# Sliding-window attention with a token mixer: two batches of natural q and k, eight sets of exponentials, held stores and a new order of work

## The chip, the core and the metric

The kernel runs on one core of a Trainium2 chip. Five engines work side by side, each through its own list of instructions in order: TensorE (PE; its weight loads are listed apart as PEld), VectorE (DVE), ScalarE (ACT), GpSimd (POOL) and SyncE (SP). They wait for each other through semaphores only. The metric is the time of one execution on the device in microseconds.

## The reference: what is computed

q, k and v are 8 batches x 8 heads x 576 positions x 64, in float32. Each head has a window of 128 positions and a slope; the attention's output, put side by side over the heads, is x (8 x 576 x 512), and x goes through a token mixer:

```python
scores = scale * np.matmul(q, k.transpose(0, 1, 3, 2))
mask = (rel >= 0) & (rel < window)
scores = np.where(mask, scores + bias[None], -1000000000.0)
...
attn = attn / (np.sum(attn, axis=-1, keepdims=True) + 1e-09)
return np.matmul(attn, v).astype(np.float32)
...
wq = x @ w_q
wk = x @ w_k
W_tok = scale * np.einsum('bsd,btd->bst', wq, wk)
mixed = np.einsum('bst,btd->bsd', W_tok, x)
return (np.maximum(mixed, 0.0) @ w_out).astype(np.float32)
```

The mixer needs the whole of a batch's x before its first product is complete.

## The kernel before

The 576 positions of a batch are four blocks of 128 and a tail of 64. The kernel is a list of small operations, each named after its kind, batch and part (QK3.1.0 is batch 3, block 1, half 0 of the heads). `ORDER` is a text written out beforehand: it gives the operations one after the other, each with its engine (P, A, D, G, S for PE, ACT, DVE, POOL, SP) and, for a PE operation, the pair of PSUM banks and the bank that it fills. Every engine gets its operations in the order of that text and runs them in that order; the framework adds the waits that the data need. The durations and start times that the operations carry in the code (`want`, `pe(...)`, `EV(...)`) were used to make the text and have no effect on a run.

The kinds, in the order in which a batch goes through them:

- Lq, Lk, Lv, Lt: loads of a block of q, of k, of v, and of the tails of two batches, with conversion to float16, issued by GpSimd (POOL). LF are the first blocks, issued by SP and ACT in float32.
- TQ (TF, TJ for batch 0; TT for tails): transposes of a block of q and k on PE; ETQ (EF, EJ, ETT) copies the result from PSUM to `qkT`, on ACT or DVE.
- QK: the scores of one block of keys for four heads, into a pair of banks; EXP (ACT) takes the exponential into a tile `pt`; MUL (DVE) multiplies it by the exponential of the bias, which holds the mask too. `NPT` is the number of sets of `pt` that are used in turn: EXP of a set waits for the products (PV) that read it last.
- PV: the product with v, whose tile has a column of ones, so that the sum comes with it; RC takes its reciprocal and X scales it into `x` (both DVE).
- XT, XTT: transposes of x and of its tails; EXT, EXTT copy them.
- For each two batches: WQ, WK, WT are the products with w_q and w_k (EWQ, EWK, EWT their copies), G is wk times x (EG), MX the mixing with RM and RMT the relu behind it, OUT the product with w_out, EO the copy of the result to a tile `osb`, and DO its store, issued by SP. There are `OSB` tiles `osb` in turn.
- wz, Lw, Lwo, CWQ, CW: wz (DVE) writes one column of the `osb` tile that w_q and w_k are then loaded into, so that SP's load Lw comes behind it; SP issues Lw (two DMAs) and Lwo, the four blocks of w_out; CWQ and CW convert them. WK and WQ need CWQ, OUT needs all CW.
- WM: matmuls on a tile of zeros whose result is not used; `WARM` holds how many of them each stands for.

The operations of a stage are mixed with those of others: while two batches go through the mixer, the next ones go through the attention. Natural q and k (`nat`) and v (`vt`) have room for four batches each; a load waits for the operation that last read what it overwrites. A load that GpSimd issues also waits for the eighth load before it.

Of the kernel before, what the change touches and what calls it, by code (L numbers as in the profile page):

```python
# [25 lines left out]
NNAT = 4  # L26
NV = 4
NPT = 5
# [13 lines left out]
EF0.1.0:D zeros:D Lk0.3:G TF0.0.0:P00 WM.2:P10 EF0.0.0:A TF0.0.1:P01 WM.3:P20 Lt0:G EF0.0.1:A  # L42
QK0.0.0:P1 TF0.1.1:P00 EXP0.0.0:A WM.4:P20 EF0.1.1:D TJ0.1.1:P01 QK0.0.1:P2 WM.5:P30 MUL0.0.0:D
# [4 lines left out]
EXP0.3.0:A MUL0.2.0:D Lv0.1:G WM.11:P01 TQ1.1:P00 EXP0.3.1:A Lq1.3:G MUL0.3.0:D WM.12:P20  # L48
ETQ1.1:D EXP0.2.1:A Lk1.3:G TQ1.0:P01 WM.13:P20 Lv0.2:G ETQ1.0:D MUL0.1.0:D QK1.0.0:P0 Lv0.3:G
QK1.0.1:P1 MUL0.2.1:D PV0.0:P2 EXP1.0.1:A WM.14:P31 Lk2.3:G MUL0.3.1:D TQ1.2:P30 EXP1.0.0:A  # L50
WM.15:P31 ETQ1.2:D Lk2.2:G PV0.1:P1 QK1.1.1:P3 RC0.1:D Lq2.2:G QK1.1.0:P0 X0.1:D EXP1.1.0:A
RC0.0:D Lv1.0:G MUL1.0.0:D TQ1.3:P10 WM.16:P11 EXP1.1.1:A ETQ1.3:D Lq2.3:G PV0.2:P0 X0.0:D
QK1.2.0:P1 Lv1.1:G PV0.3:P3 MUL1.1.0:D EXP1.2.0:A QK1.2.1:P2 MUL1.1.1:D Lv1.2:G EXP1.2.1:A
QK1.3.1:P1 RC0.2:D MUL1.0.1:D Lv1.3:G EXP1.3.1:A MUL1.2.0:D QK1.3.0:P2 Lk2.1:G X0.2:D EXP1.3.0:A
XT0.0:P10 RC0.3:D Lq2.1:G PV1.0:P0 X0.3:D EXT0.0:A MUL1.3.0:D TQ2.3:P11 Lq2.0:G TQ2.2:P20
MUL1.2.1:D ETQ2.3:A PV1.1:P3 Lk2.0:G MUL1.3.1:D XT0.1:P21 RC1.0:D PV1.2:P1 RC1.1:D Lv1.4:G
# [6 lines left out]
CW.3:A QK2.3.0:P1 EG0:D EXP2.3.0:A CW.0:D Lv2.3:G MX0.1:P0 MX0.0:P2 RM1.1:D MX0.3:P3 RM0.1:A  # L63
MX0.2:P1 Lv2.0:G RM1.3:A RM0.3:D TQ3.0:P00 RM1.0:A Lk3.3:G QK2.2.1:P3 ETQ3.0:D RM1.2:A TQ3.1:P01
EXP2.2.1:A RM0.2:D Lv2.2:G OUT1.0:P00 ETQ3.1:D RM0.0:A Lv3.0:G QK2.3.1:P1 MUL2.2.0:D QK3.0.0:P3
EXP2.3.1:A QK3.0.1:P2 MUL2.3.0:D Lk4.2:G OUT1.3:P01 MUL2.0.1:D EXP3.0.1:A OUT1.1:P10 Lk4.1:G
MUL2.3.1:D EXP3.0.0:A MUL2.2.1:D OUT0.1:P11 Lt2:G MUL2.0.0:D EO1.3:A TQ3.2:P20 EO1.0:A
MUL3.0.0:D PV2.1:P3 EO0.1:A ETQ3.2:D Lq4.2:G PV2.0:P0 DO1.0:S TQ3.3:P21 EO1.1:A RC2.1:D
OUT0.3:P11 X2.1:D Lv3.1:G ETQ3.3:A RC2.0:D PV2.3:P3 X2.0:D Lq4.1:G EO0.3:A QK3.1.0:P2 RC2.3:D
QK3.2.0:P0 X2.3:D EXP3.1.0:A Lv3.2:G PV2.2:P1 MUL3.0.1:D OUT1.2:P30 EXP3.2.0:A Lv3.3:G  # L70
MUL3.1.0:D XT2.0:P31 RC2.2:D Lv3.4:G EO1.2:A MUL3.2.0:D QK3.1.1:P2 QK3.3.0:P0 EXP3.1.1:A Lk4.3:G
X2.2:D OUT0.0:P30 EXT2.0:D Lq4.3:G EXP3.3.0:A QK3.3.1:P1 QK3.2.1:P2 EO0.0:D TT4:P31 Lq4.0:G
EXP3.2.1:A MUL3.1.1:D MX0.4:P0 OUT0.2:P30 MUL3.3.0:D RMT0:A Lk4.0:G PV3.0:P2 MUL3.2.1:D
EXP3.3.1:A TQ4.2:P00 Lv2.4:G ETT4:D TQ4.1:P01 ETT5:A RC3.0:D MUL3.3.1:D PV3.1:P1 Lq5.0:G EO0.2:A
# [36 lines left out]
EXT7.0:A DO4.0:S X6.4:D XT7.1:P01 OUT5.2:P20 RC7.4:D EXT7.1:A X7.4:D MX4.4:P3 XTT6:P21 RMT4:D
WK6:P00 EXTT6:A WT6:P01 EWK6:A WQ6:P10 EWT6:D G6:P11 EWQ6:A EO5.2:A OUT5.4:P30 EG6:D DO5.2:S
# [46 lines left out]
def kernel(  # L159
# [751 lines left out]
```

## Time and profile before

| | |
|---|---|
| time of 3 runs, median (lowest to highest) | 143.82 us (143.59 to 145.14) |
| the profiled execution's own time | 145.0 us |
| its span, first to last instruction | 143.1 us |
| PE busy; useful matmuls end | 129.3 us; 138.9 us |
| ACT busy; DVE busy; POOL busy | 118.7; 117.5; 95.3 us |
| warm matmuls | 72, 12.0 us |
| first load of GpSimd; end of its last | 2.46; 106.6 us |
| first exponential starts | 6.99 us |
| first store of a result; last one issued | 54.0; 139.6 us |

Of this profile the busy times by stretch say which engine has room in which stage, the waits say who stood for whom, the chain of work that ended last says where the end comes from, and the timeline gives the moment of a single operation. Durations of instructions that follow each other on an engine overlap by some hundredths of a microsecond, so that a sum of durations is larger than the busy time.

### The profile page before, as it was taken

The page shows a single profiled execution, that of the slowest core. Times are in us where ns is not written, and L with a number is a line of the kernel's source. Part 1 is how long each engine was busy: PE and PEld are TensorE (multiplying, and loading weights), DVE is VectorE, ACT ScalarE, POOL GpSimd, SP SyncE. Part 2 cuts the span into 40 slices and gives each one's busy share as a digit, 9 for nine tenths or more (in the row PEclk, how much of TensorE's full clock was granted, in tenths as well). Part 3 has the DMA queues.
Part 4 walks back from the last instruction along what each step waited for, and adds up shares of the span by engine and source line. Part 5 has one row for each costly group of instructions (what it writes and reads, how often), then busy time and mean ns, then how long its engine had stood idle before and what let it go on. Part 6 is the DMA issues. An engine that isn't in the chain of part 4 may idle for free.

```text
span 143.1 us, 4562 instructions
## 1 busy us (share of the span) xinstructions
PE 129.3 (90%) x1888; PEld 86.8 (61%) x1888; DVE 117.5 (82%) x253; ACT 118.7 (83%) x166; POOL 95.3 (67%) x118
## 2 busy tenths in 40 slices
PE   7979898589496999999998999999999999999980
PEld 4737776378263557678855466787665557863430
DVE  5478499988557999999879999999999999939720
ACT  4956967979398999999899999999999999867140
POOL 7999999999839999899949759998570000000000
PEclk9999999999999999999999999999999999999999
DMA  4999999999999999999999999999999941504494
GB/s 101 240 155 154 156 155 156 155 154 167 262 172 157 154 155 182 161 151 211 252 164 181 241 206 157 155 184 248 163 235 283 215 161 73 220 5 136 125 390 161
DMA packets 119333, 25.60 MB, mean 179 GB/s; under 512 B 114192, under 2 KB 114192, under 8 KB 119312
## 3 DMA queue, kind: packets, MB, share of 16 engines
q0 software_dynamic: 109264, 13.77, 151.9%
q1 hardware_dynamic: 8992, 11.28, 23.9%
q10 hardware_dynamic: 1056, 0.26, 0.8%
q8 instruction: 15, 0.25, 0.6%
q14 instruction: 6, 0.05, 0.1%
HBM read 29.62 MB, written 9.44 MB: 273 GB/s over the span
## 4 chain that ended last, share of the span: by engine, by line
PE 56%; POOL 15%; DMA 9%; DVE 7%; ACT 7%; issue 2%; SPq 0%; POOLq 0%; ACTq 0%
PE pair L232 46%; PE pair L235 11%; POOL nat L364 10%; DMA osb<-in_moe_w_k_dram 5%; DMA nat<-in_q_dram 5%; ACT pt L588 4%; POOL vt L381 3%; DVE rm L773 2%; DVE qkT L241 1%; POOL natt L371 1%; DVE osb L241 1%; DVE pt L595 1%; ACT wqT L239 1%; DVE x L635 1%; DVE wqT L241 0%
## 5 line engine op out<-in xcount | busy, mean ns | idle before, releaser
L588 ACT ACTIVATE pt<-pair 128x1024 f16<-128x1024 f32 x64 | 62.6, 1033 | 5.6 <-PE pair L232 5.1
L381 POOL DMA_DIRECT2D vt<-in_v_dram x40 | 34.7, 900 | 4.3 <-PE pair L232 2.1
L595 DVE TENSOR_TENSOR pt<-pt,bias 128x1024 f16<-128x1024 f16 x48 | 31.4, 680 | 2.9 <-ACT pt L588 2.8
L364 POOL DMA_DIRECT2D nat<-in_k_dram x31 | 28.8, 937 | 5.5 <-DMA natt<-in_k_dram 2.7
L232 PE MATMUL pair<-wout_sb,rm 128*128 128x512 f16 x128 | 31.1, 380 | 0.0
L364 POOL DMA_DIRECT2D nat<-in_q_dram x30 | 28.1, 947 | 0.7 <-PE pair L232 0.6
L232 PE MATMUL pair<-vt,pt 128*128 128x65 f16 x576 | 24.0, 193 | 1.1 <-DVE x L635 0.5
L232 PEld LDWEIGHTS <-pt 128*128 128x128 f16 x576 | 21.2, 97 | 6.3 <-issue 2.9
L232 PE MATMUL pair<-qkT 64*128 64x256 f16 (+2 forms) x320 | 21.6, 250 | 1.0 <-ACT pt L588 0.7
L635 DVE TENSOR_TENSOR x<-pair,inv 128x512 f16<-128x512 f32 x32 | 21.8, 687 | 0.8
L235 PE MATMUL pair<-identh,nat 128*128 128x128 f16 x244 | 18.6, 219 | 1.6 <-DMA nat<-in_k_dram 0.8
L239 ACT COPY osb<-pair 128x512 f32<-128x512 f32 x25 | 14.5, 609 | 5.0 <-PE pair L232 5.0
L232 PEld LDWEIGHTS <-rm 128*128 128x128 f16 x128 | 11.2, 98 | 11.7 <-issue 0.6
L235 PEld LDWEIGHTS <-nat 128*128 128x128 f16 x244 | 14.5, 97 | 5.5 <-DMA nat<-in_k_dram 1.9
L241 DVE COPY qkT<-pair 128x1024 f16<-128x1024 f16 (+1 forms) x26 | 15.2, 592 | 2.2 <-PE pair L235 1.1
L232 PEld LDWEIGHTS <-qkT 64*128 64x128 f16 x320 | 11.1, 94 | 8.5 <-issue 5.4
L239 ACT COPY qkT<-pair 128x1024 f16<-128x1024 f16 (+1 forms) x15 | 13.5, 916 | 0.9 <-PE pair L235 0.9
L232 PE MATMUL pair<-warm 128*128 128x256 f16 x72 | 12.0, 299 | 1.6 <-DVE warm L282 1.1
L239 ACT COPY xT<-pair 128x1024 f16<-128x1024 f16 x12 | 12.1, 1027 | 1.1 <-PE pair L235 0.8
L595 DVE TENSOR_TENSOR pt<-pt,biasl 128x1024 f16<-128x1024 f16 x16 | 10.8, 681 | 0.4 <-ACT pt L588 0.2
L771 ACT ACTIVATE rm<-pair 128x512 f16<-128x512 f32 x18 | 9.7, 618 | 0.6 <-PE pair L232 0.6
L235 PE MATMUL pair<-identh,x 128*128 128x128 f16 x128 | 9.6, 219 | 0.5 <-ACT pt L588 0.5
(69 smaller groups left out, 135.9 us busy)
## 6 DMA issues: line engine op xcount, KB each, us to landing
out_dram<-osb SPq DMA_DIRECT2D x32, 256.0 KB, 4.4
vt<-in_v_dram POOLq DMA_DIRECT2D x32, 128.0 KB, 6.8
nat<-in_k_dram POOLq DMA_DIRECT2D x31, 128.0 KB, 6.3
nat<-in_q_dram POOLq DMA_DIRECT2D x30, 128.0 KB, 6.5
osb<-in_moe_w_out_dram SPq DMA_DIRECT2D x4, 256.0 KB, 6.9
out_dram<-osb SPq DMA_DIRECT2D x8, 128.0 KB, 4.3
osb<-in_q_dram SPq DMA_DIRECT2D x4, 128.0 KB, 3.6
natt<-in_q_dram POOLq DMA_DIRECT2D x4, 128.0 KB, 6.1
```

Of the source, the lines that this page charges most:

```text
L232: hold(nc.tensor.matmul(*a, **k))
L235: hold(nc.tensor.transpose(*a))
L239: hold(nc.scalar.copy(out_ap, in_ap))
L241: hold(nc.vector.tensor_copy(out=out_ap, in_=in_ap))
L364: return lambda: nc.gpsimd.dma_start(out=natv(b, j, n), in_=(q, k)[j][b, :, P * n:P * n + P, :].transpose([1, 0, 2]))
L371: nc.gpsimd.dma_start(out=natt_s[pr % 2][:, j].rearrange("p e h d -> p (e h) d"), in_=(q, k)[j][2 * pr:2 * pr + 2, :, 512:576, :].rearrang ...
L381: return lambda: nc.gpsimd.dma_start(out=vtv(b, t)[:n, :, 0:D], in_=v[b, :, P * t:P * t + n, :].transpose([1, 0, 2]))
L588: nc.scalar.activation(out=pt[:, 0:1024], in_=two(s.bank).rearrange("p e c -> p (e c)"), func=AF.Exp, scale=SCALE)
L595: ENG2[o.eng].tensor_tensor(out=pt[:, 0:1024], in0=pt[:, 0:1024], in1=bt, op=ALU.mult)
L635: nc.vector.tensor_tensor(out=x[r].rearrange("p (g h d) -> p g h d", g=2, h=4), in0=sums(p)[r, :, :, 0:64], in1=box["inv"][r].unsqueeze(3) ...
L771: hold(nc.scalar.activation(out=out_ap, in_=in_ap, func=AF.Relu, scale=WSCALE))
L773: hold(nc.vector.tensor_scalar(out=out_ap, in0=in_ap, scalar1=0.0, scalar2=WSCALE, op0=ALU.max, op1=ALU.mult))
```

## The change

- Natural q and k are kept for two batches instead of four, each in tiles of its own; the tiles of v are split by batch too, and stay four. A load of q or k now waits for the transposes of the batch two before.
- There are eight sets of `pt` instead of five, and 15 tiles `osb` instead of 12.
- A new kind GT stands in the order of SP. It issues nothing: it puts a QK operation of batch 3 or later on a list, and the next store waits for all QK on that list. That holds the stores.
- The last block of the last batch is computed, copied and stored in two halves of 256 columns, as OUT7.3 and OUT7.8.
- The order is new as a whole, with another choice of engine for the copies, and there are 105 warm matmuls instead of 72. Loads of v begin later in GpSimd's order, behind all q and k of batches 0 and 1. The weights are asked for behind wz as before; the block of w_out that SP issued ahead of them no longer is.
- The mixer's code is written for groups of one or two batches; the groups are the same pairs.

Of the order, the parts about the start, the weights and the end are shown.

```diff
-NNAT = 4
+NNAT = 2
 NV = 4
-NPT = 5
+NPT = 8
 PTW = 1088
 NX = 4
 
 FIRST32 = ((0, 0), (1, 0), (0, 1))
 
-OSB = 12
+OSB = 15
 WIDE = ()
 
-WARM = (13, 8, 2, 1, 2, 1, 4, 1, 9, 2, 6, 2, 9, 7, 1, 2, 2)
+GATES = 3
+
+GROUPS = ((0, 1), (2, 3), (4, 5), (6, 7))
+GROUP = {b: g for g, bs in enumerate(GROUPS) for b in bs}
+POS = {b: e for bs in GROUPS for e, b in enumerate(bs)}
+SINGLES = [g for g, bs in enumerate(GROUPS) if len(bs) == 1]
+
+SPLIT = ((7, 3),)
+
+WARM = (13, 5, 2, 2, 8, 5, 5, 7, 5, 1, 1, 1, 18, 5, 7, 5, 7, 1, 7)
...
-warm:D LF0.0.1.1:A iota:G LF0.1.0.0:S WM.0:P01 ident:G LF0.0.1.0:A LF0.0.0.0:S wmc:D ones:D
-LF0.0.0.1:S mask:G LF0.1.0.1:S Lk0.1:G bias:A Lq0.2:G idh:D TF0.1.0:P00 WM.1:P01 Lk0.2:G
...
-Lq0.3:G EXP0.0.1:A TJ0.2.0:P00 WM.6:P30 EJ0.1.1:D Lk1.1:G EJ0.2.0:D TJ0.2.1:P10 biasl:D
-QK0.1.0:P0 WM.7:P30 Lq1.1:G TJ0.3.1:P11 QK0.1.1:P2 WM.8:P31 Lq1.0:G EXP0.1.1:A MUL0.0.1:D
-EJ0.2.1:D Lk1.0:G EXP0.1.0:A TT0:P30 EJ0.3.1:D WM.9:P20 MUL0.1.1:D Lq1.2:G TJ0.3.0:P31 WM.10:P20
-ETT0:D EJ0.3.0:A Lv0.0:G ETT1:A QK0.2.0:P0 QK0.2.1:P1 EXP0.2.0:A QK0.3.0:P2 Lk1.2:G QK0.3.1:P3
...
-pads:D EXT0.1:A wz:D X1.1:D Lwo.1:S Lv0.4:G Lw:S ETQ2.2:A X1.0:D PV1.3:P3 Lt1:G RC1.2:D Lwo.3:S
-XT1.0:P00 RC1.3:D X1.2:D Lwo.0:S QK2.2.0:P2 Lwo.2:S EXT1.0:A X1.3:D TQ2.1:P01 Lq3.0:G ETQ2.1:D
-XT1.1:P10 EXP2.2.0:A TQ2.0:P11 Lk3.0:G EXT1.1:A PV1.4:P0 ETQ2.0:D Lq3.1:G QK2.1.1:P3 RC1.4:D
-QK2.0.0:P1 X1.4:D CWQ:A PV0.4:P2 Lk3.1:G EXP2.1.1:A WK0:P00 RC0.4:D X0.4:D Lq3.3:G EXP2.0.0:A
-QK2.1.0:P3 EWK0:D QK2.0.1:P2 Lq3.2:G EXP2.1.0:A XTT0:P01 WQ0:P10 EXTT0:D Lv2.1:G EXP2.0.1:A
-MUL2.1.0:D WT0:P11 Lk3.2:G MUL2.1.1:D TT2:P00 EWT0:A EWQ0:A CW.1:D G0:P01 ETT2:A ETT3:D CW.2:D
...
-EXP7.3.0:A PV7.0:P0 OUT4.0:P11 MUL7.3.1:D EO5.0:A RC7.0:D PV7.1:P2 X7.0:D EO4.0:A DO5.0:S
...
-DO7.2:S EO6.1:D OUT6.3:P31 DO6.1:S EO6.2:A OUT7.3:P10 DO6.2:S EO6.3:A DO6.3:S EO7.3:A DO7.3:S
...
+warm:D LF0.0.0.0:S LF0.0.1.0:A iota:G WM.0:P01 ident:G wmc:D LF0.0.1.1:A LF0.1.0.0:S ones:D
+mask:G LF0.1.0.1:S LF0.0.0.1:S Lq0.2:G bias:A Lk0.1:G pads:D TF0.0.0:P00 Lk0.2:G WM.1:P10
+zeros:D TF0.1.0:P01 WM.2:P11 Lq0.3:G EF0.1.0:A biasl:D TF0.1.1:P10 WM.3:P20 EF0.0.0:A
+TF0.0.1:P11 Lk0.3:G QK0.0.0:P0 EF0.0.1:A WM.4:P20 EXP0.0.0:A Lk1.2:G EF0.1.1:D idh:D QK0.0.1:P1
...
+EJ0.3.1:D Lk1.1:G QK0.2.0:P3 MUL0.1.0:D WM.11:P21 EXP0.1.1:A TQ1.2:P20 Lk2.2:G WM.12:P21
+EXP0.2.0:A MUL0.1.1:D Lq2.2:G ETQ1.2:A MUL0.2.0:D Lk1.0:G MUL0.2.1:D TT0:P00 Lq1.0:G WM.13:P21
+ETT0:D QK0.3.0:P1 Lv0.1:G QK0.3.1:P2 EXP0.3.0:A TQ1.3:P01 Lv0.2:G WM.14:P30 ETQ1.3:D EXP0.3.1:A
+ETT1:D Lv0.0:G QK1.2.1:P1 MUL0.3.0:D QK1.2.0:P3 EXP1.2.1:A QK1.3.1:P0 Lv0.3:G TQ1.1:P20
...
+Lv1.2:G ETQ1.0:D MUL1.1.1:D EXP1.1.0:A QK1.0.1:P2 Lk2.0:G PV0.2:P1 MUL1.3.1:D WM.17:P31
+EXP1.0.1:A Lv1.1:G RC0.2:D PV0.0:P0 MUL1.3.0:D PV0.1:P3 X0.2:D Lv1.3:G PV0.3:P2 RC0.1:D
...
+EXP2.2.0:A Lv0.4:G MUL1.2.0:D XT0.1:P20 Lt1:G EXP2.2.1:A XT0.0:P21 RC1.0:D wz:D X1.0:D Lw:S
+PV1.1:P3 EXT0.1:D EXT0.0:A PV1.3:P1 Lwo.0:S Lwo.2:S PV1.2:P0 RC1.1:D Lk3.0:G RC1.3:D Lwo.3:S
...
+RC0.4:D QK2.1.0:P3 X0.4:D EXP2.1.1:A Lk3.2:G QK2.0.1:P0 MUL2.2.0:D XTT0:P10 CWQ:A Lv2.2:G
+QK2.0.0:P2 CW.2:D EXP2.1.0:A WK0:P11 EXTT0:D EXP2.0.0:A MUL2.1.0:D WT0:P10 WQ0:P30 EWK0:D EWT0:A
+EXP2.0.1:A G0:P31 CW.1:D Lk3.3:G CW.3:A MUL2.0.0:D TT2:P10 EWQ0:D EG0:A Lq3.3:G CW.0:A
...
+QK3.1.1:P2 Lv3.1:G MUL2.3.0:D QK3.1.0:P0 DO0.3:S EXP3.1.1:A QK3.0.1:P3 GT3.1:S OUT0.2:P10
...
+EXP7.3.0:A PV6.3:P1 MUL7.1.1:D OUT4.3:P31 RC6.3:D EO4.2:A X6.3:D EO4.0:A PV7.1:P2 MUL7.3.0:D
...
+DO6.2:S EO7.0:A OUT7.2:P21 DO7.0:S EO6.0:A OUT7.8:P01 DO6.0:S EO7.2:A OUT7.3:P31 EO7.8:A DO7.2:S
+EO7.3:D DO7.3:S DO7.8:S
...
-    nat_s = [[[cpool.tile([P, 2, H, D], F16, name=f"nat{i}{j}{n}") for n in range(4)]
-              for j in range(2)] for i in range(2)]
+    nat_s = [[[cpool.tile([P, H, D], F16, name=f"nat{i}{j}{n}") for n in range(4)]
+              for j in range(2)] for i in range(NNAT)]
...
-    vt_s = [[cpool.tile([P, 2, H, VW], F16, name=f"vt{i}{t}") for t in range(5)] for i in range(2)]
+    vt_s = [[cpool.tile([P, H, VW], F16, name=f"vt{i}{t}") for t in range(5)] for i in range(NV)]
...
-        return nat_s[(b // 2) % 2][j][n][:, b % 2]
+        return nat_s[b % NNAT][j][n]
 
     def vtv(b, t):
-        return vt_s[(b // 2) % 2][t][:, b % 2]
+        return vt_s[b % NV][t]
...
-        for i in range(2):
-            nc.vector.memset(vt_s[i][4][64:128], 0.0)
-            for t in vt_s[i]:
-                nc.vector.memset(t[:, :, :, D:D + 1], 1.0)
+        for vt_b in vt_s:
+            nc.vector.memset(vt_b[4][64:128], 0.0)
+            for t in vt_b:
+                nc.vector.memset(t[:, :, D:D + 1], 1.0)
...
+            loads[b, j, n] = load(("L" + "qk"[j], b, n), next(i), [dma_nat(b, j, n)], 1,
+                                  tq.get((b - NNAT, n, j), []))
...
+        if u == 0 and b >= GATES:
+            add("GT", b, g, w, {"SP": (0.02, 0.02)}, [s], lambda o: gates.append(s))
...
+    def gated(i):
+        while gates:
+            tc.add_manual_dep(
+                i.ins, gates.pop().insts[-1].name,
+                mybir.DependencyInfo(mybir.DependencyClass.Sync, mybir.DependencyReason.DATA),
+                reason="stores behind loads")
...
+        if (b, st) in SPLIT:
+            add_out_cols(b, st, want, 0, 256, st)
+            add_out_cols(b, st, want, 256, 512, st + 5)
+        else:
+            add_out_cols(b, st, want, 0, DM, st)
...
+            cp(o.eng, box["o"][0:rows, c0:c1], one(t.bank)[0:rows, 0:c1 - c0])
...
+                gated(nc.sync.dma_start(out=out[b, P * st:P * st + P, c0:c1], in_=osb))
```

More of the change, by code (lines that the diff above doesn't have):

```diff
@@ L50 @@
[L50 to L55, printed above, removed]
@@ L193 @@
     xtl_s = [cpool.tile([P, DM], F16, name=f"xtl{i}") for i in range(2)]
+    xone_s = [cpool.tile([P, DM], F16, name=f"xone{i}") for i in range(len(SINGLES))]
     xT_s = [cpool.tile([P, 4, DM], F16, name=f"xT{i}") for i in range(NX)]
@@ L323, in mk_pads @@
     def mk_pads(o):
+        for t in xone_s:
+            nc.vector.memset(t[64:128], 0.0)
         for t in wkt_s:
@@ new lines, in add_mix, with ev1 @@
+        mxd[gi, db] = t
+        prev = GROUPS[gi - 2] if gi >= 2 else ()
+        if db < 4 and nb == 1:
+            old = [osd.get((x, st)) for x in prev for st in range(4)]
+            def ev1(o):
+                relu(o.eng, rm_s[sl][:, db, 0, :].rearrange("p (e t) -> p e t", e=2),
+                     two(t.bank)[:, :, 0:256])
+            erm[bs[0], db] = add("RM", bs[0], db, want + 0.4, EV(0.60, 0.69), [t, *old], ev1, frees=[t])
+        elif db < 4:
+            old = [osd.get((x, st)) for x in prev for st in range(4)]
+            for e, b in enumerate(bs):
@@ L818, in add_out @@
         need = [*wto]
-        need += [erm[b // 2, db, b % 2] for db in range(4)] if st < 4 else [erm[b // 2, 4]]
-        t = add("OUT", b, st, want, pe(0.86), need, em, banks=1)
-        osd[b, st] = t
+        need += [erm[b, db] for db in range(4)] if st < 4 else [erm[gi, "t"]]
+        t = add("OUT", b, part, want, pe(0.86 * (c1 - c0) / DM), need, em, banks=1)
+        osd[b, part] = t
         box = {}
```

328 lines of the change are left out of this document (161 added, 167 removed).

## The prediction, made before the result was known

> **What bounds the kernel now.** I read the page's first part, then busy time by stretch, then the waits and the chain where a stretch has a hole, then the tail.
>
> ```profile
> span 143.1 us, 4562 instructions
> ...
> PE 129.3 (90%) x1888; PEld 86.8 (61%) x1888; DVE 117.5 (82%) x253; ACT 118.7 (83%) x166; POOL 95.3 (67%) x118
> ```
>
> ```profile
> core 0: us, PE busy (x) PEld busy (x) DVE busy (x) ACT busy (x) POOL busy (x), PEclk, DMA share, GB/s
> 40.00:50.00 10.00, 8.63 (x123) 4.91 (x121) 8.04 (x15) 9.38 (x17) 8.15 (x10) 1.00 2.39 157
> 50.00:110.00 60.00, 59.41 (x957) 40.93 (x952) 57.43 (x110) 58.30 (x82) 49.15 (x58) 1.00 2.14 195
> 110.00:120.00 10.00, 9.99 (x132) 5.97 (x131) 9.86 (x20) 10.00 (x14) 0.00 (x0) 1.00 0.86 158
> 118.80:125.00 6.20, 6.20 (x126) 4.90 (x124) 5.74 (x15) 5.76 (x8) 0.00 (x0) 1.00 0.44 169
> ```
>
> From 50 to 120 us three engines are full at once: PE 69.4 of 70 us, ACT 68.3, DVE 67.3. A new order can win at most ACT's 1.7 us there. The rest of the lost time lies before 50 us and after 120.
>
> Before 50 us there is one hole in which all three stop. The waits name it and the chain shows where it comes from:
>
> ```profile
> ACT wqk_sb L239 <- DMA osb<-in_moe_w_k_dram: 2.4, 1, 2.4
> DVE wk L241 <- PE pair L232: 2.2, 1, 2.2
> PE pair L232 <- ACT wqk_sb L239: 2.1, 1, 2.1
> ```
>
> ```profile
> 31.51 0.37 SPq L441
> ...
> 31.92 6.73 DMA osb<-in_moe_w_k_dram
> 38.65 0.02 issue
> 38.67 0.63 ACT wqk_sb L239
> 39.30 0.04 issue
> 39.34 1.66 PE pair L232 x40
> ```
>
> The projection weights are asked for only when DVE reaches wz (31.42); CWQ follows 7.25 us later, and WK0, the first projection, at 39.34. Ahead of that GpSimd sets the pace: its first load starts at 2.46 us and its 31st at 28.77, so one every 0.877 us. The median load of q or k lands 6.4 us after its issue, of v 6.8.
>
> **The change, part by part.** *Work.* I added up each order by the mean durations of the groups of before (EXP 1.033, MUL 0.680, X 0.687, ETQ 1.033 on ACT or 0.685 on DVE, OUT 0.86 and so on), up to the same operations; I leave the warm matmuls out. After minus before: up to G0 ACT +0.5, DVE +1.0 (all of it new memsets: ten of 0.072 for v's ones, six for pt at a distance of 0.045); from G0 to X7.4 ACT +0.2, DVE -0.2, PE 0; in all ACT +2.3, DVE -1.1, PE 0. The extra on ACT mostly falls behind G6, where ACT is idle anyway (8.1 busy of 11.0 from 120 to 131, 3.0 of 8.0 from 131 to 139). So the middle costs 0. Its bounds are ACT's and DVE's idle of 50 to 110 us: -1.7 if the new order closes all of ACT's, +2.6 if it opens as much again as DVE's.
>
> *Start.* The new order loads q and k of batches 0 and 1 ahead of v: the v blocks that the first product (PV0.2) needs are loads 18 and 19, not 13. Load 19 starts at 2.46 + 18 x 0.877 = 18.2 and lands at 25.0; before, the first product ran at 19.84. What this gives is exponentials: eight sets instead of five let ACT run all sixteen of batches 0 and 1, and three of batch 2, ahead of CWQ (before: one). What it costs is on DVE, which gets X and RC of both batches only from PV0.2's end, 25.0 + 0.65 = 25.7. Between there and wz it has five MUL, four X, five RC; at the distances in the trace (two MUL in 1.28, X 0.63, RC 0.15) that is 6.5, so wz is at 32.2, 0.8 later than before. CWQ follows 7.25 later at 39.5, WK0 at 40.1. DVE's CW.2 now stands ahead of EXTT0 and EWK0 and waits for the fourth DMA behind wz, which is issued after three others (0.37, 0.51 and a third of 2.14) at 33.9 and lands, by the 6.9 of w_out's row, at 40.8; then 0.5 for CW.2, 0.42 EXTT0, 0.68 MUL2.1.0, 0.69 EWK0: G0 at 43.1, where before had 43.26. It is 0.2 earlier with 0.5 more of ACT's work done: -0.7. Bounds: -2.4, if nothing of the hole is left; +2.6, if the weights land as late as the load of 31.81, which GpSimd waited for until 41.73 (9.9 us, 3.0 over 6.9).
>
> *Warm matmuls.* 105 instead of 72. The early rows give a price:
>
> ```profile
> 1.06 2.95 PE L232 MATMUL pair<-warm 128*128 128x256 f16 x13 [1.06 <-DVE warm L282]
> ...
> 11.52 1.16 PE L232 MATMUL pair<-warm 128*128 128x256 f16 x9
> ```
>
> Thirteen took 0.22 each at first, nine later 0.11. The 33 more are 3.6 us of PE ahead of 29 us, where PE's useful rows are some 17 of 39 us; the longest block, 18 ahead of TT0, is 2.0 us and can hold the last exponentials of batch 0 back by about 1. ACT regains that while it waits for load 19, so 0; without that cover +1. Beside this: the Trainium skill, TensorE: Matmul & The Clock Gate, Part 1, has the array start at half rate until some 3.4 us of activity, and fall back after as long idle. The two rows agree, although PEclk says 1.00 in both; by its cold price the 18 would cost 3.9 and TT0 would be 2 us later, but the longest wait of PE in this trace is 2.1.
>
> *Two batches of q and k.* A load of batch b+2 waits for TQ of batch b. The first of batch 4 is load 46, 41.9 at the earliest, and TQ2.0 is done by 35; batch 7's first is at 80.5 or later, with TQ5.0 around 79. GpSimd ended at 106.6 with PE busy to 138.9, so 0; if the queue stood 1.5 at TQ5.0, still 0.
>
> *Held stores.* SP alone waits, and behind a held store are only other stores. I count at most 7 result tiles unstored at once in either order, of 12 before and 15 after, so no copy waits for a tile: 0. What stores cost the loads is bounded by what PE's matmuls and weight loads waited for DMA after 40 us, 0.6.
>
> *Behind the last exponential.* Up to EXP7.3.0 ACT's sum is the same (+0.1), but PE has done 1.2 less: eight PV and four XT are still to come where it was six and three. ACT is at 10.00 of 10 from 110 to 120, so it cannot get there sooner by itself; from 118.8 to 125 PE is at 6.20 of 6.20, so what is left queues on PE. I take +1.2; bounds 0 (PE set the pace before 118.8 too, at 9.99) and 1.4.
>
> *Last block in halves.*
>
> ```profile
> 138.97 0.58 ACT L239 COPY osb<-pair 128x512 f32<-128x512 f32 x1 [0.28 <-PE pair L232]
> 139.59 0.33 SPq L833 DMA_DIRECT2D out_dram<-osb  x1
> ```
>
> ```profile
> out_dram<-osb SPq DMA_DIRECT2D x32, 256.0 KB, 4.4
> ...
> out_dram<-osb SPq DMA_DIRECT2D x8, 128.0 KB, 4.3
> ```
>
> The last copy shrinks from 0.58 to some 0.42 (the row of a 128x256 copy on DVE), -0.2; a second store adds an issue of 0.33. Half the bytes save between 0.1 (4.4 against 4.3 us to landing) and 1.6 (half of the 3.2 us from the end of the last issue to the end); I take the row, 0.1. Together 0; bounds -1.5 and +0.1. The Trainium skill, DMA: Bandwidth & Descriptors, Anatomy of one DMA, speaks against the halving: about 2 us of a DMA is fixed, and bytes go at 436 GB/s. By it a half saves 0.3 and the sum would be 0.2 lower; the 0.1 of this case's two rows is on its side.
>
> *Sum:* -0.7 + 0 + 1.2 + 0 = +0.5. The profiled execution took 145.0 (span 143.1 and 1.9 around), 1.2 over the median of 143.82; it would become 145.5, and the median **144.3**.
>
> **Rivals.** *Faster, 141.4.* The weights arrive when ACT reaches CWQ, with three exponentials of batch 2 already behind it: the hole's 2.4 goes, and ACT carries the lead to the end, so that the last exponential comes 1.2 sooner and PE's longer queue behind it costs nothing: 143.8 - 2.4. For it: ACT is 2.0 of row time further at CWQ than before. Against: of that lead 0.5 is left at G0, so most of it is order, not time.
>
> *Slower, 146.7.* DVE is the new bound around the weights. CW.2 stands in front of EXTT0 and EWK0; each microsecond that its w_out block lands past 40.8 moves G0 by one, and with it the last exponential. Four 256 KB loads now share this stretch (before three; one had come at 2.9). Price: +1.7 of the +2.6 bound in place of -0.7, with +1.2 behind the last exponential: 143.8 + 1.7 + 1.2. It decides from a wz at 33 us on, which whole durations instead of distances (7.2 in place of 6.5) would nearly give.
>
> *No effect, 143.8.* The stages are full whatever the order: ACT's and DVE's sums are the same, and stores were late before too (DO1.3 stands 143 operations behind its copy already).
>
> **Chances.** My forecast with the no-effect case, 0.41; the faster rival, 0.25; the slower, 0.34, as two of my terms (1.2 at the end, the weights) have more room up than down. A measurement of this kernel tells about 1% (1.4 us) from no change. The range, from 141.0 to 147.2, takes in both rivals and half a microsecond more each way; all of -1.5 at the end and all of +2.6 in the middle together with a rival are the 2 in 10 left out.
>
> **What the profile of after would show.** First PV near 25.0 (before 19.84); wz near 32.2 and WK0 near 40.1; a wait of DVE at CW.2 of one to two us; G0 near 43. From 50 to 110 us ACT between 57.5 and 59. More than 6.0 us from the last exponential to XTT6: about 7.2. Last copy 0.4, and two stores behind it. I am wrong if PV comes late by more than 2 us against 25, if ACT falls under 56 of 60 in the middle, or if result copies wait for stores.

## The result and the profile after

The changed kernel takes **144.38 us** (median of 20 runs, 143.68 to 146.16) where the kernel before takes 143.66 on the same chip (20 runs, 142.16 to 145.61). The ratio is **1.0064**, 95% interval 1.0037 to 1.0090: slower by 0.9 us, within the 1% that a measurement of this kernel can tell. The ratio leaves out slow runs, those over 1.5% above the fastest of their kernel, and the profiled execution of the kernel before (145.0 us, 1.3 over the median) was one of them, so that a difference of a microsecond between the two traces need not come from the change. The forecast was 144.3. Whether its terms were right is another matter; the experiments answer it in part.

The profiled execution of the changed kernel took 145.19 us, with a span of 143.4. The first part of its page:

```profile
span 143.4 us, 4657 instructions
...
PE 132.9 (93%) x1925; PEld 90.0 (63%) x1925; DVE 114.5 (80%) x266; ACT 120.2 (84%) x172; POOL 95.4 (66%) x118
```

PE is busy 3.6 us longer than before. Its warm matmuls alone took 16.7 us where they had taken 12.0, so PE's useful work did not grow. Busy time by stretch (columns: the stretch, its length, then busy time and instructions of each engine):

```profile
40.00:50.00 10.00, 8.07 (x108) 4.69 (x104) 8.20 (x16) 8.26 (x16) 6.62 (x9) 1.00 2.21 183
50.00:110.00 60.00, 59.26 (x952) 39.56 (x950) 55.52 (x107) 58.82 (x83) 49.52 (x58) 1.00 2.20 192
110.00:120.00 10.00, 9.93 (x138) 6.15 (x138) 9.61 (x21) 9.57 (x15) 0.00 (x0) 1.00 0.68 181
117.60:124.80 7.20, 7.20 (x148) 5.78 (x147) 6.84 (x16) 6.26 (x9) 0.00 (x0) 1.00 0.58 219
```

From 50 to 110 us PE does what it did before (59.26 against 59.41) and ACT a little more (58.82 against 58.30). The last row is the stretch from the last exponential to XTT6: it is 7.2 us long where it was 6.0, and PE is full in it, as forecast. But it begins 1.2 us sooner: the last exponential ends at 117.56 (before 118.77) and XTT6 starts at 124.79 (before 124.82). In these two traces the longer queue has cost nothing.

Around the weights the waits read (who waits, for whom: us in total, times, longest):

```profile
DVE wout_sb L257 <- DMA osb<-in_moe_w_out_dram: 2.7, 2, 1.9
PE pair L248 <- DVE xTt L257: 1.2, 1, 1.2
```

and the chain of waits (start, us, what):

```profile
32.35 0.04 DVE osb L437
32.38 0.02 issue
32.40 0.37 SPq L442
...
35.52 8.22 DMA osb<-in_moe_w_out_dram
43.73 0.02 issue
43.76 0.43 DVE wout_sb L257
...
45.44 0.82 PE pair L248 x6
```

ACT's wait for w_k, 2.4 us before, is gone. In its place VectorE stands at CW.2 (1.93 us, until 41.06) and at CW.1 (until 43.76), and PE waits 1.2 us for EXTT0, which stands behind CW.2. So the hole has changed hands. The operations came where the prediction had put them: first PV 25.69 (25.0), wz 32.30 (32.2), CWQ 38.86 (39.5), WK0 39.53 (40.1), VectorE at CW.2 until 41.06 (40.8), G0 43.11 (43.1).

At the end the last copy is a half, as forecast, and the two half stores land a little sooner than the whole ones beside them (timeline, and DMA issues from 134 us on with the size and the median us to landing):

```profile
139.02 0.42 DVE L257 COPY osb<-pair 128x256 f32<-128x256 f32 x1 [3.69 <-ACT osb L255]
```

```profile
out_dram<-osb SPq DMA_DIRECT2D x7, 256.0 KB, 2.1
out_dram<-osb SPq DMA_DIRECT2D x2, 128.0 KB, 1.9
```

Over the whole execution the stores of 128 KB take 2.5 us in the median and those of 256 KB 4.9, but eight of the ten of 128 KB are stores of tails at other moments; the halves alone gain 0.2. The last copy ends at 139.44 (before 139.55), yet the span ends at 143.4 (before 143.1): SP issues the store of the last half only at 140.32, 0.84 us after that of the half before it.

### The profile page after: what moved, and what is told of

Same layout as the page of the kernel before. It is cut to its first block, busy times and chain, and to the rows that moved or that the text cites. A ratio compares the mean times of both kernels' runs of the same rounds, so it can differ in the third digit from the quotient of the medians.

```text
span 143.4 us, 4657 instructions
## 1 busy us (share of the span) xinstructions
PE 132.9 (93%) x1925; PEld 90.0 (63%) x1925; DVE 114.5 (80%) x266; ACT 120.2 (84%) x172; POOL 95.4 (66%) x118
## 4 chain that ended last, share of the span: by engine, by line
PE 68%; ACT 10%; DVE 8%; DMA 6%; issue 3%; SPq 2%; DVEq 0%
PE pair L248 54%; PE pair L251 13%; DMA osb<-in_moe_w_out_dram 6%; ACT pt L591 5%; DVE pt L598 3%; ACT rm L785 2%; DVE x L638 2%; ACT xT L255 1%; SPq L442 1%; DVE qkT L257 1%; SPq L450 1%; DVE osb L257 1%; ACT wqT L255 1%; DVE inv L652 0%; DVE rm L787 0%
## 5 line engine op out<-in xcount | busy, mean ns | idle before, releaser
L248 PE MATMUL pair<-wout_sb,rm 128*128 128x512 f16 (+1 forms) x132 | 31.2, 373 | 0.4 <-ACT rm L785 0.4
L378 POOL DMA_DIRECT2D nat<-in_k_dram x31 | 30.0, 973 | 1.5 <-DMA vt<-in_v_dram 0.6
L248 PE MATMUL pair<-vt,pt 128*128 128x65 f16 x576 | 22.6, 193 | 0.0
L248 PEld LDWEIGHTS <-rm 128*128 128x128 f16 x132 | 11.5, 97 | 12.3 <-issue 1.0
L248 PE MATMUL pair<-warm 128*128 128x256 f16 x105 | 16.7, 299 | 1.1 <-DVE warm L298 1.1
L255 ACT COPY osb<-pair 128x512 f32<-128x512 f32 (+1 forms) x24 | 13.9, 614 | 3.4 <-PE pair L248 3.2
L255 ACT COPY qkT<-pair 128x1024 f16<-128x1024 f16 (+1 forms) x16 | 14.3, 926 | 1.4 <-PE pair L251 1.4
L257 DVE COPY osb<-pair 128x512 f32<-128x512 f32 (+1 forms) x13 | 8.6, 667 | 8.0 <-PE pair L248 4.2
L248 PEld LDWEIGHTS <-warm 128*128 128x128 f16 x105 | 10.6, 107 | 3.8 <-DVE warm L298 1.1
L255 ACT COPY xT<-pair 128x1024 f16<-128x1024 f16 x11 | 11.1, 1022 | 1.2 <-PE pair L251 1.2
L785 ACT ACTIVATE rm<-pair 128x512 f16<-128x512 f32 x20 | 10.9, 629 | 0.6 <-PE pair L248 0.6
```

What stands on the lines that cost most here:

```text
L248: hold(nc.tensor.matmul(*a, **k))
L255: hold(nc.scalar.copy(out_ap, in_ap))
L257: hold(nc.vector.tensor_copy(out=out_ap, in_=in_ap))
L378: return lambda: nc.gpsimd.dma_start(out=natv(b, j, n), in_=(q, k)[j][b, :, P * n:P * n + P, :].transpose([1, 0, 2]))
L785: hold(nc.scalar.activation(out=out_ap, in_=in_ap, func=AF.Relu, scale=WSCALE))
```

## The experiments

All twelve were timed in five rounds against the kernel before, which ran beside them. They ran four at a time, each four on a chip of its own, so that between such groups the ratios compare and the times less well. None leaves out any of the computation. Three questions were open: which part of the change costs the 0.6%, why the forecast's two large terms (-0.7 and +1.2) came out as they did, and which engine sets the pace. In the expectations, "theory 1" and so on belong to that run alone.

### The last block whole; the halves in turn

```diff
-SPLIT = ((7, 3),)
+SPLIT = ()
...
-OUT7.8:P01
...
-EO7.8:A
...
-DO7.8:S
```

> The changed kernel with its last block whole: OUT7.8, EO7.8 and DO7.8 go, OUT7.3 is 512 columns wide again. In the profile of the changed kernel the last copy ends 0.11 us sooner than before (139.44 against 139.55) but the span ends 0.3 later, with the second half's store issued at 140.32, 0.84 after the first. Theory 1 (the halves cost): 0.3 to 0.4 us faster than the changed kernel, ratio to the kernel before near 1.003. Theory 2 (halves cost nothing, my term of 0): within 0.1 us of the changed kernel.

```diff
-EO7.3:D DO7.3:S DO7.8:S
+DO7.8:S EO7.3:D DO7.3:S
```

> The changed kernel with the stores of the two halves in the order in which the copies end (DO7.8 ahead of DO7.3). Theory 1 (it is the second store, standing behind the later copy, that ends the span): its issue moves from 140.32 to some 139.0, the last issue is DO7.3 at 139.8, and the time falls by 0.5 us. Theory 2 (the landing of a store ends it, wherever it stands): less than 0.2 us.

Whole: 144.23 us, ratio 1.0050 [1.0016, 1.0084]. Halves with the store of the half that is copied first also issued first: 144.29, ratio 1.0066 [1.0028, 1.0104]. Both intervals hold the changed kernel's 1.0064. In turn, the last store is issued 0.58 us behind the last copy instead of 0.87, and the time shows nothing of it. The halves are worth nothing that can be measured, in either order of their stores.

### The buffers alone; holding in the old order

The order and the warm matmuls of the kernel before, in the changed kernel's code and buffers (two batches of natural q and k, eight sets of `pt`, 15 `osb`), no holding, no halves:

```diff
-GATES = 3
+GATES = 8
-SPLIT = ((7, 3),)
+SPLIT = ()
-ORDER, WARM = (changed kernel)
+ORDER, WARM = (kernel before)
```

> The order and the warm matmuls of the kernel before, with the buffers of the changed one (natural q and k for two batches, eight sets of exponentials, 15 result tiles, tiles of v by batch), no held stores, the last block whole. Theory 1 (buffers alone do nothing, the order is the change): within 0.3 us of the kernel before. Theory 2 (five sets or the shared tiles held the old order back): 0.5 us or more faster than before. Theory 3 (two batches of q and k hold GpSimd back): 0.5 us or more slower.

The same with a GT behind each first half of QK from batch 3 on:

```diff
-GATES = 8
+GATES = 3
...
+GT3.0:S
```

> The old order on the new buffers, as in the run of that name, with held stores added: each GT directly behind its QK of batches 3 to 7. Taking the holding from the new order cost some 1 us, with PE waiting 1.2 us for q of batch 4 or so between 60 and 70 us. Theory 1 (the gain belongs to the new order, which reads batch 4 sooner than its loads bear): within 0.3 us of the old order without holding. Theory 2 (holding helps any order): 0.5 us or more faster than it.

The buffers alone: 143.82 us, ratio 1.0012 [0.9972, 1.0052]. With GT: 144.25, ratio 1.0052 [1.0013, 1.0090]. The second run was meant to tell whether holding helps the old order too. It can't: the stores of the two kernels start at the same moments (51.6, 61.9, 62.4, 62.8, 63.3, 71.9 against 51.6, 62.0, 62.4, 62.8, 63.3, 71.9 us), because in the old order each store stands behind the scores that the new wait asks for. So it is nearly the same kernel measured twice, and 0.4% is what two such measurements can differ by. The changed kernel's 0.6% over before is clear of zero in its twenty runs; how much of it is the buffers (0 to 0.5%) and how much the order can't be settled from the times. On the chip of the first of these two runs the new order reads 1.0050 and 1.0066 against 1.0012; on the chip of the second it reads 1.0053 (next but one section) against 1.0052, which is no difference. The traces can say more about where the orders differ.

### Where the order loses: the start

I compare the run with the old order (buffers alone) with the run of the new order with the last block whole. In both PE reached full speed at about the same moment (4.8 and 4.4 us; why that matters comes at the end). Busy time from 0 to 41 us, and that of the warm matmuls alone in the same stretch, first of the old order, then of the new:

```profile
0.00:41.00 41.00, 35.38 (x532) 27.71 (x532) 31.65 (x107) 32.52 (x44) 38.87 (x53) 1.00 2.09 172
...
0.00:41.00 41.00, 12.31 (x72) 7.41 (x72) 0.17 (x1) 1.00 2.09 172
```

```profile
0.00:41.00 41.00, 37.08 (x547) 29.18 (x549) 31.45 (x108) 31.94 (x41) 39.69 (x53) 1.00 2.03 168
...
0.00:41.00 41.00, 16.00 (x105) 10.20 (x105) 0.17 (x1) 1.00 2.03 168
```

PE looks busier with the new order, but less the warm matmuls it has done 21.1 us of work against 23.1. What is late is what waits for v. The first PV, WK0 and G0 of the old order, then of the new (timeline of PE):

```profile
19.01 0.43 PE L242 MATMUL pair<-vt,pt 128*128 128x65 f16 x8
...
37.12 1.09 PE L242 MATMUL pair<-wqk_sb,xT 128*128 128x64 f16 x32 [0.41 <-ACT wqk_sb L249]
...
41.03 1.05 PE L242 MATMUL pair<-x,wk 128*64 128x512 f16 x8
```

```profile
24.76 0.66 PE L244 MATMUL pair<-vt,pt 128*128 128x65 f16 x16
...
38.61 1.09 PE L244 MATMUL pair<-wqk_sb,xT 128*128 128x64 f16 x32
...
41.69 1.03 PE L244 MATMUL pair<-x,wk 128*64 128x512 f16 x8
```

Between the first PV and WK0 stands wz, at 30.26 and 31.37. Part of the delay is made up by G0, and the rest is carried: G4 102.98 against 102.34, last result copied 137.98 against 137.50. So in this pair the new start costs 0.5 to 0.7 us.

This pair alone does not show the ratio's 0.6%. Its execution of the new order took 143.05 us, 1.2 under the median of its kernel, and its span is the shorter one (141.3 against 141.6), since its last store lands sooner. The other traces say more. In the six whose start is that of the changed kernel, G0 starts at 41.69 to 43.37 us, 42.5 in the mean; in the three with the old start in the new buffers (buffers alone, with GT, and the old start with the new rest, below) at 41.03, 41.12 and 41.89, 41.3 in the mean. From G0 to the last copy it takes 96.2 to 96.3 us with the new order (changed kernel, last block whole, halves in turn) and 96.3 to 96.5 with the old (kernel before, buffers alone, with GT). So what differs between the orders differs ahead of G0, by an estimate of 1.1 us from these few executions. That this makes up the ratio is not shown, since on the chip of the run with GT the times do not tell the two orders apart.

### Fewer warm matmuls

```diff
-WARM = (13, 5, 2, 2, 8, 5, 5, 7, 5, 1, 1, 1, 18, 5, 7, 5, 7, 1, 7)
+WARM = (13, 1, 1, 1, 8, 5, 5, 7, 5, 1, 1, 1, 5, 5, 7, 5, 7, 1, 7)
```

> The changed kernel with 1, 1, 1 warm matmuls instead of 5, 2, 2 between the first transposes, and 5 instead of 18 ahead of TT0. In the profiles so far PE's warm matmuls go from 0.21 to 0.11 us each somewhere between 4.1 and 6.9 us, a different moment in each execution; when it is late, the five ahead of the second transposes cost 1.07 instead of 0.55 and the first exponential comes at 8.0 to 8.3 instead of 7.0. Theory 1 (warm matmuls stand in the way at the start): first exponential at 6.5 to 7.5 whatever the moment, the last of batch 0 one microsecond sooner, the time 0.3 to 0.6 us shorter. Theory 2 (v's arrival at 25 sets the pace): the exponentials come sooner, the first product does not, time within 0.2 us.

144.06 us, ratio 1.0053 [1.0012, 1.0094]. Nineteen useless matmuls fewer bring nothing that can be measured. The first exponential starts at 7.66 us, later than theory 1 had it. Whatever PE gains by them ends in the same hole; VectorE's waits of this run, from 28 to 60 us:

```profile
DVE wout_sb L257 <- DMA osb<-in_moe_w_out_dram: 3.1, 2, 2.3
```

2.3 us at the longer of the two where the changed kernel's had 1.9.

### Weights asked for sooner

If the weights come late, why not ask sooner? In the changed kernel wz, Lw and Lwo were put behind ETQ1.0; in the kernel before behind X0.1 (there Lwo.1 stays where it was):

```diff
-ETQ1.0:D
+ETQ1.0:D wz:D Lw:S Lwo.0:S Lwo.2:S Lwo.3:S Lwo.1:S
```

> The changed kernel with wz and the loads of all weights moved up behind ETQ1.0, to some 25.5 us instead of 32.3. In the profile of the changed kernel DVE waits 2.7 us for blocks of w_out and PE 1.25 behind it. Theory 1 (the late weights are what the new order loses at its start, and the later stages carry each microsecond to the end): G0 1 to 1.5 us sooner, the time 1 us or more shorter than the changed kernel, ratio to before under 1.000. Theory 2 (the weights' 1.3 MB then push v and q and k of batch 2): first product and transposes of batch 2 later by a microsecond or more, no gain. Theory 3 (the middle, not the start, sets the time): G0 sooner, the end where it was.

```diff
-X0.1:D
+X0.1:D wz:D Lw:S Lwo.3:S Lwo.0:S Lwo.2:S
```

> The kernel before with the same move: wz and the weights' loads behind X0.1, at some 23 us instead of 31.4. There ACT waited 2.4 us for w_q and w_k, and all three engines stood. Theory 1: 1 to 2 us faster than before (ratio 0.986 to 0.993). Theory 2 (contention with loads): no gain. Theory 3: the hole closes, the end stays.

146.85 us, ratio 1.0250 [1.0191, 1.0309], and 146.66, ratio 1.0218 [1.0155, 1.0281]. Against the kernel before they lose 2.5 and 2.2%, and the first loses 1.9% against the changed kernel, so it is no gain in either order. The waits say for what. In the changed kernel with sooner weights (20 to 50 us):

```profile
PE pair L244 <- DMA vt<-in_v_dram: 2.6, 1, 2.6
```

and in the kernel before with sooner weights:

```profile
PE pair L232 <- DMA nat<-in_q_dram: 2.8, 1, 2.8
PE pair L229 <- DMA vt<-in_v_dram: 1.5, 1, 1.5
```

The weight DMAs run beside the loads, and these land late: from 20 to 35 us the median for q is 9.5 us in the first run, where the changed kernel's is 5.0, and PE stands still for 2.6 and 4.3 us. At neither of these two places is there room for up to 1.3 MB of weights (two DMAs of 128 KB, four of 256) without something else being late.

### The cast of w_out later

```diff
-QK2.0.0:P2 CW.2:D EXP2.1.0:A
+QK2.0.0:P2 EXP2.1.0:A
...
-CW.1:D
+CW.1:D CW.2:D
```

> The changed kernel with VectorE's cast of the third part of w_out moved behind that of the second, so that VectorE does not wait for its DMA (1.93 us in the profiled execution) ahead of the eviction that the first pair's product needs. Theory 1 (that wait is on the path: TensorE waits 1.2 us behind that eviction): 0.5 to 1.2 us shorter than the changed kernel, ratio 0.998 to 1.003. Theory 2 (TensorE's own queue is late by then and the wait moves to the next cast): ratio 1.004 to 1.008.

145.14 us, ratio 1.0126 [1.0072, 1.0181]. No gain; the interval overlaps that of the changed kernel, so that a loss is not shown either. Yet the wait ahead of G0 did go: G0 starts at 41.53 instead of 43.11, though the exponentials ahead of it run only 0.3 us sooner. From 28 to 75 us, VectorE and PE of this run:

```profile
DVE wout_sb L253 <- DMA osb<-in_moe_w_out_dram: 1.1, 1, 1.1
...
PE pair L244 <- DVE wqT L253: 1.6, 1, 1.6
```

Now PE waits 1.6 us for the copy of WQ, which stands behind CW.2 on VectorE. The 24th exponential ends 0.5 us sooner (52.01 against 52.52), and 0.3 of it were there at the first. So of 1.6 us won at G0 some 0.2 are left.

### Stores not held

All GT are taken out of the order.

```diff
-GATES = 3
+GATES = 8
...
-GT3.1:S
```

> The changed kernel without the GT operations: stores wait only for their copies and for their place in SP's order. My prediction priced the holding at 0: within 0.2 us of the changed kernel. Rival 1 (holding keeps loads fast): slower by 0.5 to 1 us, with GpSimd's waits for DMA longer. Rival 2 (held stores crowd the end): faster by 0.3 us or more.

145.41 us, ratio **1.0133** [1.0087, 1.0179], against 1.0050 [1.0016, 1.0084] of the new order with the last block whole, in the same rounds. Halves in turn, which keeps the halves as this run does, had 1.0066 [1.0028, 1.0104]. In this order holding is worth about 1 us. First the stores issued by SP (timeline, 45 to 82 us), then busy time from 60 to 70 us, without holding:

```profile
48.45 11.49 SPq L869 DMA_DIRECT2D out_dram<-osb  x7
64.06 1.18 SPq L872 DMA_DIRECT2D out_dram<-osb  x2
```

```profile
60.00:70.00 10.00, 8.27 (x168) 6.97 (x164) 8.33 (x19) 8.65 (x12) 6.80 (x8) 1.00 1.92 230
```

and in the changed kernel:

```profile
49.94 30.70 SPq L875 DMA_DIRECT2D out_dram<-osb  x7
80.73 1.19 SPq L878 DMA_DIRECT2D out_dram<-osb  x2
```

```profile
60.00:70.00 10.00, 9.77 (x209) 8.45 (x209) 9.31 (x21) 9.66 (x14) 9.09 (x12) 1.00 2.24 189
```

Seven stores lie in 11.5 us instead of 30.7. The loads that run beside them land later (from 45 to 75 us the medians are 9.6 us for q and 8.7 for k, with held stores and the last block whole 7.1 and 7.3), GpSimd gets through 6.8 us of issuing instead of 9.1, and PE loses 1.5 us of these ten. Its waits in this run, 50 to 75 us, name the load:

```profile
PE pair L245 <- DMA nat<-in_q_dram: 1.2, 1, 1.2
PE pair L245 <- DMA nat<-in_k_dram: 0.5, 1, 0.5
```

From G0 to G2 it takes 31.9 us, with held stores (last block whole) 30.4. GpSimd's last load ends at 110.4 instead of 106.1. Without holding the new order would have lost 1.3%, not 0.6%.

### Who sets the pace from 50 us on

27 more warm matmuls (2.9 us of PE) in the full stretch, nine each ahead of TQ5.1, TQ6.0 and XT4.1:

```diff
-WARM = (..., 1, 7)
+WARM = (..., 1, 7, 9, 9, 9)
...
+WM.19:P11
...
+WM.20:P00
...
+WM.21:P21
```

> The changed kernel with 27 more warm matmuls (three groups of 9, at 0.108 us each 2.9 us of TensorE's time, useless work) ahead of a transpose of q of batch 5, a transpose of q of batch 6 and a transpose of x of batch 4, at about 76, 87 and 92 us. Theory 1 (TensorE sets the pace from 41 us to the end: it is busy 99% of that stretch, and the end follows the TensorE work left at 41 us): the time is 2.5 to 3 us longer, ratio to the kernel before 1.024 to 1.028. Theory 2 (ScalarE and VectorE set the pace and TensorE's busy time is partly matmuls spread out by waits): below 1 us, ratio 1.006 to 1.013.

Three copies moved from VectorE to ScalarE (3.1 us of ACT):

```diff
-ETQ5.1:D   ETQ6.3:D   EXT5.1:D
+ETQ5.1:A   ETQ6.3:A   EXT5.1:A
```

> The changed kernel with three evictions of 128x1024 (q of batch 5, first pair; q of batch 6, last pair; x of batch 5, second half) given to ScalarE instead of VectorE: ScalarE +3.1 us (three by 1.03), VectorE about -2.1 us, between 76 and 97 us, TensorE unchanged. Theory 1 (TensorE sets the pace): within 0.5 us of the changed kernel, ratio 1.003 to 1.010, and ScalarE's last exponential ends 1 to 3 us later than 117.6. Theory 2 (ScalarE sets the pace): 2 to 3 us longer, ratio 1.020 to 1.028.

147.01 us, ratio 1.0265 [1.0227, 1.0303], and 146.87, ratio 1.0244 [1.0193, 1.0295]: by the ratios 2.9 and 2.6 us over the changed kernel, by the times 2.6 and 2.5. In each pair of theories I had made one engine the bound. Both additions cost nearly their whole length, so both engines are. From 70 to 110 us, the changed kernel, then with more warm matmuls, then with more on ACT (PE is the first busy time, ACT the fourth):

```profile
70.00:110.00 40.00, 39.49 (x620) 25.53 (x618) 36.36 (x69) 39.18 (x59) 31.55 (x38) 1.00 2.18 194
```

```profile
70.00:110.00 40.00, 39.92 (x592) 26.41 (x588) 33.92 (x65) 36.71 (x54) 30.74 (x37) 1.00 2.19 192
```

```profile
70.00:110.00 40.00, 38.33 (x593) 25.06 (x589) 32.84 (x62) 39.57 (x57) 30.68 (x37) 1.00 2.18 193
```

Where PE gets more to do, ACT empties (39.18 to 36.71); where ACT gets more, PE does (39.49 to 38.33). The work is so tightly interleaved that neither has the slack to take up even 3 us spread over 20.

### The old start with the new rest

```diff
-ORDER = (changed kernel)
-WARM = (changed kernel)
+ORDER = (kernel before, up to G0 and EG0) + (changed kernel, what is left)
+WARM = (kernel before)
```

> The changed kernel with the order of the kernel before up to the product G0 of the first pair (its evictions included, and its warm matmuls), and from there on the new order, held stores and halves as in the changed kernel. Theory 1 (the new start loses 0.6 to 0.7 us of TensorE's work done by 41 us, the rest of the order is worth nothing either way): as the old order in the new buffers, ratio 0.998 to 1.003. Theory 2 (the new rest gains what the new start loses): 0.5 us or more below the kernel before, ratio 0.993 to 0.997. Theory 3 (the new rest needs the lead that the new start gives in natural q and k): as the changed kernel or slower, 1.006 or above.

146.08 us, ratio 1.0158 [1.0096, 1.0221]: worse than either order in one piece. Behind the seam, from 41 to 50 us:

```profile
41.00:50.00 9.00, 6.18 (x73) 3.33 (x71) 8.21 (x16) 6.71 (x14) 7.77 (x10) 1.00 2.42 156
```

PE does 6.2 of 9 us there, where the old order in one piece does 7.8, and ACT 6.7 instead of 8.5. A reading that fits, but that no run tests, is that the new rest takes for granted what the new start has put ready, and uses later what the old start has put ready instead. So the time of this run does not isolate the start; that the start is where the new order loses rests on the traces above. No version here beats the kernel before.

## Why the prediction was right, and where it was not

The time was right (144.3 against 144.38), but by the traces two of its terms were wrong and cancelled. That the figure fits so closely is luck.

- **Work, 0: right.** PE and ACT spend the same in the middle, and from G0 to G6 it takes 84.07 us (before 83.95). The two added loads show what "full" means: a real increase of 3 us on either engine showed as 2.6 to 2.9.
- **Start, -0.7: wrong in sign, some +0.5 to +1.** Each moment of the changed kernel was forecast within 0.7 us, wz, VectorE's wait and G0 within 0.3. What failed is the subtraction: G0 at 43.1 was set against 43.26 of one execution of the kernel before, one that took 1.3 us more than the median. VectorE's moment at CW.2 came out by two errors that cancelled: the load of that block was issued at 34.57, not 33.9, and landed 6.5 us later, not 6.9. The same order ran G0 at 41.03 in the buffers' run, where the q, k and v loads of the first 30 us land after 4.8 to 4.9 us (before: 5.6 to 6.0). Like against like, the new start is 0.5 to 0.7 us behind in the pair of traces, and 1.1 in the means.
- **Warm matmuls, 0: right.** With 19 fewer the time stays. By the Trainium skill's half rate (TensorE: Matmul & The Clock Gate, Part 1) the prediction's estimate for the 18 ahead of TT0 was 3.9 us. They took 2.1 in the changed kernel, so they ran at full speed.
- **Two batches of q and k, 0: right** as far as 0.4% can be told (ratio 1.0012).
- **Held stores, 0: wrong as a step.** The bound of 0.6 was taken from where the stores stood before, and it was added up short: behind 40 us the weight loads waited 0.6 for loads of v and 0.6 for loads of k, 1.2 together. In the new order the stores would have come at 48 to 60 us, beside loads that are needed soon, and cost 1 us; holding takes that away again. The sum of the two is 0, but neither part is.
- **Behind the last exponential, +1.2: wrong, about 0.** The queue was as long as forecast, 7.2 against 6.0, in the changed kernel and in both runs on its last block alike. "ACT cannot get there sooner by itself" was the error: it was 0.5 us of work ahead at G0 by the prediction's own sum, and was 0.5 us busier from 50 to 110; the last exponential ended 1.2 sooner, and PE reached XTT6 at the same moment. The other traces agree: from G0 to the end of the last exponential it is 74.2 to 74.5 us in the new order and 75.5 to 75.7 in the old. The bound of 0 named the reason (PE set the pace before 118.8 too), and I should have taken it.
- **Last block in halves, 0: right.** Undone, or in turn, it makes no difference. The half stores land 0.2 us sooner than the whole ones beside them, but the last one is issued 0.84 us behind the other. The row of 0.1 that the prediction took was a difference of medians over the whole execution, where the 128 KB stores are tails. The saving by the Trainium skill's rule (DMA: Bandwidth & Descriptors, Anatomy of one DMA), which that section gives for DMAs issued by GpSimd while SP issues these, is 0.3 by an estimate from its figures. The 0.2 of this trace is near it, and either is within what the times can't tell.
- **The rivals.** The faster one's first condition held, as ACT's 2.4 us at CWQ did go, and so did its last, a final exponential 1.2 sooner with no cost from the queue behind it; but VectorE's 1.9 at CW.2 came in place of the hole, and G0 came only 0.15 sooner. The slower one had the place right, and the price wrong: wz came at 32.3, under the 33 from which it decides, and taking that wait away gains nothing. The case of no effect lies just outside: the lower end of the interval is 1.0037.

## What to carry to other kernels

A difference of half a percent can't be read by subtracting two single profiles whose starts were drawn differently: line up runs by an early event that the change doesn't touch, or look at the same order twice, before signing a term. In a stretch where two engines were both at 98%, an added 3 us on either cost nearly its length, and a wait that was removed came back at the next thing its engine did; look for the stretch that is not full. When work is reordered, ask anew which transfers run side by side: stores that were harmless where they stood can cost a microsecond where they land.

## What the runs showed of the hardware

**The moment at which PE gets fast differs by almost 3 us between executions.** All kernels here begin with the same 13 warm matmuls (timeline of PE; start, us, count), but the next five take 1.27 us together in the changed kernel and 0.71 in the run with the last block whole:

```profile
1.06 2.96 PE L248 MATMUL pair<-warm 128*128 128x256 f16 x13 [1.06 <-DVE warm L298]
...
4.66 1.27 PE L248 MATMUL pair<-warm 128*128 128x256 f16 x5
```

```profile
1.06 2.96 PE L244 MATMUL pair<-warm 128*128 128x256 f16 x13 [1.06 <-DVE warm L294]
...
4.48 0.71 PE L244 MATMUL pair<-warm 128*128 128x256 f16 x5
```

From 4.0 us (kernel before), 4.4 (last block whole), 6.4 (changed kernel) or 6.8 (halves in turn) on, warm matmuls and the transposes between them start 0.11 us apart instead of 0.21: 2.9 to 5.7 us after the first. Where that comes at 6.4 or later the first exponential starts at 8.0 to 8.3 us (at 7.7 with fewer warm matmuls), where it comes at 4.0 to 4.4 at 6.9 to 7.1. In the new order the delay is not made up: between the run with the last block whole and that with the halves in turn it is 1.23 us at the first exponential and 1.24 at the last copy. In the old order most of one was: between the buffers alone and the run with GT it is 0.58 us at the first exponential, 0.09 at G0 and 0.06 at the last copy. The granted clock in the profile reads 1.00 all the while. The Trainium skill (TensorE: Matmul & The Clock Gate, Part 1) calls the window free-running and the release run-variable, by half a microsecond about 4 us. The moment varies here too, with a wider spread; whether a free-running window is why, no run shows.

**After a wait of 2.6 us PE's clock was halved for 3.4 us.** In the changed kernel with sooner weights PE stands still from 32.1 to 34.7 us; busy time by microsecond (PE first; the granted clock is the number behind the engines):

```profile
33.00:34.00 1.00, 0.00 (x0) 0.00 (x0) 0.02 (x1) 0.47 (x1) 0.00 (x0) 1.00 2.07 198
34.00:35.00 1.00, 0.28 (x10) 0.28 (x10) 0.00 (x0) 0.00 (x0) 0.03 (x1) 1.00 2.33 164
35.00:36.00 1.00, 0.85 (x26) 0.76 (x23) 0.21 (x1) 0.00 (x0) 0.78 (x1) 0.86 2.48 153
36.00:37.00 1.00, 1.00 (x23) 1.00 (x21) 0.61 (x2) 0.00 (x0) 1.00 (x2) 0.50 2.41 153
...
39.00:40.00 1.00, 1.00 (x27) 1.00 (x25) 0.69 (x1) 0.60 (x2) 1.00 (x2) 0.93 2.41 154
```

The clock falls a microsecond after PE has resumed, and stays at 0.50 until 39.1; eight transposes take 1.04 us there instead of 0.61. So the price of this late transfer is, by estimate, those 2.6 and the 1.7 that PE loses in 3.4 us at half speed. The same page of the Trainium skill has the rule that the clock falls after a gap of over some 3.4 us. Here it fell after 2.6, with PE busy only 0.76 to 0.97 of the time in the 6 us before it. In the kernel before with sooner weights it fell at 28.1 us, in the middle of a gap of 1.5, with PE busy for 1.75 of the 4 us up to 28, and stayed at 0.50 until 34.9; and the kernel before stood for 2.1 us from 37.3 on with the clock at 1.00. So the length of one gap does not decide alone. What else does is open: no run changed the gap alone.
